# Attention scores of a head pair in two pieces instead of three, inside a fused attention and MLP kernel

## The chip, the cores and the metric

The kernel runs on one core of one Trainium2 chip. The metric is the device time of one execution in microseconds (us). The kernel before was timed three times: 943.04, 944.19 and 946.74 us, median 944.19 us.

## What is computed

The reference is causal attention with a window of 128 and a linear (ALiBi) bias, followed by an MLP with GELU:

```python
# q, k, v: 8 batches, 8 heads, 576 positions, 64 wide;  x: 4608 x 512
scores = scale * np.matmul(q, k.transpose(0, 1, 3, 2))
rel = pos[:, None] - pos[None, :]
bias = slopes[:, None, None] * (-np.abs(rel).astype(np.float32))[None, :, :]
mask = (rel >= 0) & (rel < window)
scores = np.where(mask, scores + bias[None], -1000000000.0)
scores = scores - np.max(scores, axis=-1, keepdims=True)
attn = np.exp(scores)
attn = attn / (np.sum(attn, axis=-1, keepdims=True) + 1e-09)
x = np.matmul(attn, v)          # reshaped to tokens x 512
h = x @ w_in                    # 512 x 2048
out = gelu(h) @ w_out           # 2048 x 512
```

## The kernel before

**Tiles.** The 4608 tokens are nine MLP tiles of 512. Every product is done in fp16 as a high and a low part, three matmuls for one. Tile `t` of the MLP is 32 steps: in steps 0 to 15 `mlp_in` forms one h of 128 features (12 matmuls of 512 columns, L600), the Activation engine (ACT) takes its GELU (L623), GpSimd (POOL) writes the high part (L625) and VectorE (DVE) the low part (`low_part`, L149); in steps 16 to 31 `mlp_out` forms a quarter of an output block `o` (again 12 matmuls, L661). The h and o tiles rotate through four PSUM buffers with the tag "mm". TensorE (PE) is kept on these products, and the attention of the next batch, `b = t + 1`, is threaded between the steps.

**Attention units.** A batch has four units, one for each pair of heads (0 to 3). A unit's scores need nine blocks of 64 rows per half, kept as nine groups in five PSUM banks (`BANKS`): (0, 1), (2, 3), (4,), (5, 6), (7, 8). A bank is called by its first group. Banks 0, 2 and 4 are the EVEN groups (five of them), banks 5 and 7 the ODD ones (four). A bank with two groups takes 12 matmuls of 64 x 64 by 192 columns, bank 4 takes 6 (L415). Each matmul uses one quadrant of the array: the head chooses the rows, the half the columns; bank 4 holds a group of both heads, one per half.

**What follows a score bank.** `scores` evicts each bank to SBUF on DVE, scaled and with the bias (L437), and POOL masks its head with a memset (L442). `softmax` does the EVEN groups, then the ODD ones: the row maximum on DVE (`nmax`, L507), one exponential per group on ACT (L510, given a priority by `EXP_AHEAD`; it needs another activation table than GELU, so a table load stands before and after each run of them), then on DVE the sum made ready (`z`, L513) and its reciprocal (L514), the high part of each group on POOL (`e_main`, L519), its low part on DVE (L149), and a transposing DMA to `et`. `weigh` multiplies `et` with v on PE (L559) into two PSUM tiles `av` (one for each MLP tile that the batch overlaps), and each is read by ACT (high part of x, L572) and by DVE (low part of x, L149).

**PSUM.** Score banks and `av` tiles rotate through four buffers with the tag "att", in the order in which they are allocated: a tile takes the buffer of the tile allocated four before it, and its first matmul waits until that one has been read for the last time.

**Order.** Units 0 to 3 of a batch begin their scores at the steps `SCORES_AT = (2, 11, 16, 21)`, and `weigh` follows at `WEIGH_AT = (12, 20, 25, 30)`. The scores are issued in three pieces (`PIECES`): banks 0 and 2 at step s, bank 4 at s + 1, banks 5 and 7 at s + 2, and then the softmax. In unit 0 of batches 3 to 6, step 6 issues `stat_v` for the next batch (L217, one long DVE reduction over v) and the scale computations after it (L119 to L144, DVE). The code gives the program order only. The framework's scheduler then orders the queue of each engine by its own model of time, so a change on PE also moves DVE, ACT, POOL and the DMA queue. Names such as `sc5_3_4` read: scores of batch 5, unit 3, bank 4; `av5_1_5` is the `av` of batch 5, unit 1, for MLP tile 5; `g32_2_6` is the GELU of tile 2, h 6.

Of the kernel before, what the change touches and what calls it, by code (L numbers as in the profile page):

```python
# [51 lines left out]
BANKS = ((0, 1), (2, 3), (4,), (5, 6), (7, 8))  # L52
IDLE = {0: 6, 5: 4}
PIECES = (slice(0, 2), slice(2, 3), slice(3, 5))


@with_exitstack
def attention_gelu_mlp(
# [15 lines left out]
    def small(shape, name, bufs, tag=None, dt=F32):  # L74
        return pool.tile(shape, dt, tag=tag or name, name=name, bufs=bufs)
# [231 lines left out]
    def load_v(b):  # L307
        v32 = pool.tile([P, NPAIR, NKB, P], F32, tag="v32", name=f"v32_{b}", bufs=1)
        for hp in range(NPAIR):
            nc.sync.dma_start(v32[:, hp], vp[b, hp].rearrange("(n p) d -> p n d", p=P))  # L310
        v32s[b] = v32
# [21 lines left out]
    def split_v(b):  # L333
        v32 = v32s.pop(b).rearrange("p h n d -> p (h n d)")
        hi = vbuf[:, 0].rearrange("p h n d -> p (h n d)")
        lo = vbuf[:, 1].rearrange("p h n d -> p (h n d)")
        nc.scalar.activation(hi, v32, AF.Copy, scale=scv[b])  # L337
        low_part(lo, v32, scv[b], hi)
# [44 lines left out]
    def bias_of(hp, head):  # L383
        return bias_p[:, hp : hp + 1, :] if head is None else bias_h[:, 2 * hp + head : 2 * hp + head + 1, :]

    def scores(st, banks):

        b, hp, u = st.b, st.hp, st.u
        if not hasattr(st, "s"):
            st.ps = {}  # L390
            st.s = pool.tile([P, NG, W], F32, tag="s", name=f"s{u}", bufs=2)
        s = st.s
        exact = b < EXACT
        terms = (None,) if exact else ((0, 0), (1, 0), (0, 1))

        def operands(term, r, j):
            q, k = slice(hp * S + j * QB, hp * S + (j + 1) * QB), slice(hp * S + PAD + (j - 2) * QB, hp * S + PAD + (j + 1) * QB)
            if exact:
                return qbuf32[r, q], kbuf32[r, k]
            return qbuf[r, term[0], q], kbuf[r, term[1], k]  # L400

        ps = st.ps
        for bank in banks:
            tag = "mm" if b == 0 and bank[0] in FIRST_MM else "att"
            ps[bank] = psum.tile([P, 2, 256], F32, tag=tag, name=f"sc{u}_{bank[0]}", bufs=4)
        for n in range(len(banks[0])):
            for i, term in enumerate(terms):
                for half in range(2):
                    for bank in banks:
                        head, j = GROUPS[bank[n]]  # L410
                        h = half if head is None else head
                        jj = j if head is None else j + 2 * half
                        r, o = slice(h * D, h * D + D), slice(half * D, half * D + D)
                        a, m = operands(term, r, jj)
                        nc.tensor.matmul(  # L415
                            ps[bank][o, n, 0:W], a, m, start=(i == 0), stop=(i == len(terms) - 1 and b > 0),
                            skip_group_check=True,
                        )
            if b == 0:
                for bank in banks:  # L420
                    adds = [(slice(0, W), ident, bias_of(hp, GROUPS[bank[n]][0])[:, 0])]
                    gap = (2 - GROUPS[bank[n]][1]) * QB
                    if gap > 0:

                        adds.append((slice(0, gap), upper, never[:, 0:gap]))
                    for i, (c, a, m) in enumerate(adds):
                        nc.tensor.matmul(
                            ps[bank][:, n, c], a, m, start=False, stop=(i == len(adds) - 1), skip_group_check=True
                        )
        if b == 0:  # L430
            return
        cs = csq[b]
        for bank in banks:
            head, k = GROUPS[bank[0]][0], len(bank)
            j = GROUPS[bank[0]][1]
            bias = bias_of(hp, head)
            nc.vector.scalar_tensor_tensor(  # L437
                out=s[:, bank[0] : bank[0] + k, :], in0=ps[bank][:, 0:k, 0:W], scalar=cs,
                in1=bias.broadcast_to([P, k, W]) if k > 1 else bias, op0=ALU.mult, op1=ALU.add,
            )  # L440
            if j < 2:
                nc.gpsimd.memset(s[0:D, bank[0], 0 : (2 - j) * QB], NEG)  # L442
# [136 lines left out]
    def tile_scales(t, ns):  # L579


        k = len(ns)
        r = slice(ns[0], ns[-1] + 1)
        gs = small([P, k], f"gs{t}_{ns[0]}", 4 if t == 0 else 2, tag=f"gs{k}")
        nc.vector.tensor_scalar(gs, pww[:, r], pwx[t], 2.0 ** -(24 if t >= FAST else 25), op0=ALU.mult, op1=ALU.mult)
        sg = small([P, k], f"sg{t}_{ns[0]}", 4 if t == 0 else 2, tag=f"sg{k}")
        nc.vector.tensor_scalar(sg, sww[:, r], sx[t], 2.0 ** -(22 if t >= FAST else 21), op0=ALU.mult, op1=ALU.mult)
        for n in ns:
            gsc[t, n], gsg[t, n] = gs[:, n - ns[0] : n - ns[0] + 1], sg[:, n - ns[0] : n - ns[0] + 1]
# [50 lines left out]
    def out_scale(t):  # L640
        so[t] = small([P, 1], f"so{t}", 2, tag="so")
        nc.vector.tensor_scalar(so[t], pwm, pwx[t], 2.0 ** -(14 if t >= FAST else 16), op0=ALU.mult, op1=ALU.mult)
# [101 lines left out]
    def sums_in_place():  # L744

        for d in range(NWP // 2):
            nc.sync.dma_start(wi[2 * d + 1][:, :, 0 : NCC : 2], stored[T1, d])
        for n in (T2, T3, T4):
            stream(n, 0)
# [216 lines left out]
    def unit(b, hp):  # L966
        if (b, hp) not in units:
            units[b, hp] = Unit(b, hp)
        return units[b, hp]

    def all_scores(st):
        for piece in PIECES:
            scores(st, BANKS[piece])
# [71 lines left out]
    scores_at, weigh_at, split_at = {1: 2, 4: 3}, {5: 0, 8: 1, 11: 2, 15: 3}, {1: 2, 3: 4, 5: 6}  # L1045
# [22 lines left out]
    for t in range(1, NTILE):  # L1068
        b = t + 1
        scores_at, weigh_at = (SCORES_AT, WEIGH_AT) if t > 1 else ((8, 14, 18, 22), (17, 22, 26, 30))  # L1070
        at = {s + i: (hp, i) for hp, s in enumerate(scores_at) for i in range(3)}
        tile_scales(t, range(NWP))
        out_scale(t)
        if t == FAST:
            seven_all(t)
            break
        for step in range(2 * NFC):
            if step < NFC:
                mlp_in(t, step)
            else:  # L1080
                tb, q = divmod(step - NFC, 4)
                for fc in range(4 * q, 4 * q + 4):
                    mlp_out(t, tb, fc)
            if t + 1 == FAST:
                if step in PARTS_AT:
                    parts.pop(0)()
                if step == NFC:
                    sums_in_place()
                if step in SUMS_AT:
                    sums_of_x(FAST, SUMS_AT.index(step))  # L1090
            if b >= B:
                continue
            if step in at:
                hp, i = at[step]
                scores(unit(b, hp), BANKS[PIECES[i]])
                if i == 2:
                    softmax(unit(b, hp))
            if step == 1:
                split_v(b)
                if b + 1 < B:  # L1100
                    load_v(b + 1)
                    load_qk(b + 1)
            if step == 6:
                if b + 1 < B:
                    stat_v(b + 1)
                else:

                    pwx[B] = pwv[B - 1]
                    sx[B] = small([P, 1], f"sx{B}", 3, tag="sx")
                    inverse(sx[B], pwx[B], 12)  # L1110
                    cx_last = small([P, 1], "cxl", 1)
                    nc.vector.tensor_scalar(cx_last, pwv[B - 1], sx[B], 2.0 ** -27, op0=ALU.mult, op1=ALU.mult)
            if step in weigh_at:
                weigh(unit(b, weigh_at.index(step)))
            if step == SCORES_AT[-1] + 3 and b + 1 < B:
                split_qk(b + 1)
        if t + 2 == FAST:
            room_for_sums()
            for n in range(4):

                parts.pop(0)(gate=unit(b, NPAIR - 1).z[:, NG - 1 : NG] if n < 2 else None)
# [36 lines left out]
```

## Time and profile before

| | before |
|---|---|
| median of three runs | 944.19 us |
| profiled execution | 947.36 us, its span 945.3 us |
| mean granted TensorE clock | 0.984 |
| PE busy | 909.2 us, 96% of the span |
| DVE busy | 720.3 us, 76% |
| ACT busy | 546.5 us, 58% |
| POOL busy | 194.2 us, 21% |
| score matmuls L415 | 1656, 74.3 us of PE's busy time |

All times below are microseconds from the span's start, as the profiled execution has them. A row of the timeline gives start, duration, engine, line, operation, what it writes and reads, shapes, the count of equal neighbours put into one row, and in square brackets the engine's idle time before it with what ended it. A row of windows gives, for a stretch of time, its length, the busy time of each engine, the clock that TensorE was granted, and the share and rate of the DMA engines. The profile drops the buffer numbers, so `s<-sc` is any eviction of a score bank.

### The profile page before, as it was taken

The numbers are of one execution on the slowest core, as the hardware profiler recorded it, in microseconds if no ns is written. First come the engines' busy times: TensorE is split into PE (matmuls) and PEld (weight loads), VectorE is DVE, ScalarE is ACT, GpSimd is POOL, SyncE is SP. The second block draws the span as 40 slices with busy tenths as digits, with TensorE's granted clock in tenths as the row PEclk, the third lists the DMA queues.
The fourth block names the chain that finished last, engine by engine and source line by source line (L and its number), as shares of the span: only waits on it lengthen the run. The fifth ranks groups of instructions, "written<-read, shape, count | busy, mean of one in ns | idle before, by whom it ended". The sixth has DMA issues, their size and how long they took to land.

```text
span 945.3 us, 18563 instructions
## 1 busy us (share of the span) xinstructions
PE 909.2 (96%) x7356; PEld 475.2 (50%) x7356; DVE 720.3 (76%) x1445; ACT 546.5 (58%) x1146; POOL 194.2 (21%) x412
## 2 busy tenths in 40 slices
PE   6969999789999899999999999999999999999998
PEld 3544444444454345444454445444544444445887
DVE  6798989779876877678767877787656799991771
ACT  5977967776673565356435643564465526731760
POOL 1010000013101443135313531163125420000000
PEclk9889999999999999999999999999999999999999
DMA  9518532972446124614562346225302554300201
GB/s 317 212 45 259 209 105 67 203 191 61 90 126 165 36 57 83 187 43 79 96 162 68 62 101 174 69 51 99 86 13 51 91 116 146 90 34 23 79 24 45
DMA packets 185527, 99.63 MB, mean 105 GB/s; under 512 B 133344, under 2 KB 165216, under 8 KB 185312
## 3 DMA queue, kind: packets, MB, share of 16 engines
q1 hardware_dynamic: 185440, 98.45, 41.3%
q8 instruction: 57, 0.93, 0.4%
q14 instruction: 30, 0.25, 0.1%
HBM read 50.72 MB, written 13.63 MB: 68 GB/s over the span
## 4 chain that ended last, share of the span: by engine, by line
PE 68%; DVE 7%; ACT 5%; DMA 4%; issue 2%; SPq 1%; DVEq 0%; ACTq 0%
PE o L661 31%; PE h L600 22%; PE av L559 4%; PE sc L415 4%; DMA v<-vp 2%; PE u L789 2%; PE u_out L901 2%; PE v L789 2%; DMA et<-e_main 1%; ACT s L510 1%; DVE stv L217 1%; DVE vbuf L149 1%; DVE nmax L507 1%; ACT L623 1%; ACT vbuf L337 1%
## 5 line engine op out<-in xcount | busy, mean ns | idle before, releaser
L600 PE MATMUL h<-x,wi 128*128 128x512 f16 x1536 | 344.7, 382 | 6.5 <-ACT g L623 3.0
L661 PE MATMUL o<-wo,g 128*128 128x512 f16 x1080 | 244.7, 379 | 1.1 <-DVE wo L149 1.1
L600 PEld LDWEIGHTS <-wi 128*128 128x128 f16 x1536 | 148.2, 98 | 188.0 <-issue 14.2
L661 PEld LDWEIGHTS <-g 128*128 128x128 f16 x1440 | 136.0, 98 | 164.6 <-issue 3.0
L510 ACT ACTIVATE s<-s,nmax 128x192 f32<-128x192 f32 x252 | 111.2, 443 | 103.1 <-DVE nmax L507 99.5
L623 ACT ACTIVATE g<-h,gs 128x512 f32<-128x512 f32 x112 | 74.8, 685 | 81.0 <-PE h L600 57.4
L149 DVE SCALAR_TENSOR_TENSOR g<-g,sg,g 128x512 f16<-128x512 f32 (+1 forms) x128 | 101.9, 811 | 22.6 <-POOL g L625 19.4
L625 POOL TENSOR_SCALAR g<-g,sg 128x512 f16<-128x512 f32 x96 | 78.5, 823 | 193.4 <-ACT g L623 189.6
L149 DVE SCALAR_TENSOR_TENSOR e_main<-s,z,e_main 128x192 f16<-128x192 f32 x252 | 107.4, 469 | 14.1 <-POOL e_main L519 9.6
L519 POOL TENSOR_SCALAR e_main<-s,z 128x192 f16<-128x192 f32 x180 | 87.6, 506 | 85.4 <-ACT s L510 29.0
L415 PE MATMUL sc<-kbuf,qbuf 64*64 64x192 f16 (+1 forms) x1656 | 74.3, 261 | 9.8 <-DMA kbuf<-kp 4.5
L661 PE MATMUL o<-wo_first,g 128*128 128x512 f16 x360 | 83.2, 380 | 0.3 <-DMA wo_first<-wo 0.3
L437 DVE SCALAR_TENSOR_TENSOR s<-sc,cs,bias_h 128x384 f32<-128x384 f32 x112 | 63.7, 607 | 12.8 <-PE sc L415 12.6
L507 DVE TENSOR_REDUCE nmax<-s 128x5 f32<-128x960 f32 (+1 forms) x56 | 58.5, 1044 | 2.2 <-POOL s L442 0.2
L442 POOL MEMSET s<- 64x128 f32 (+1 forms) x112 | 19.2, 172 | 186.4 <-DVE s L437 185.7
L572 ACT ACTIVATE x<-av,cx 128x448 f16<-128x448 f32 (+6 forms) x52 | 23.6, 474 | 58.4 <-PE av L559 58.2
L415 PEld LDWEIGHTS <-qbuf 64*64 64x64 f16 x1512 | 35.9, 106 | 38.2 <-issue 35.5
L559 PE MATMUL av<-et,vbuf 128*64 128x128 f16 (+1 forms) x1680 | 45.2, 213 | 4.2 <-DMA et<-e_main 4.2
L559 PEld LDWEIGHTS <-vbuf 128*64 128x64 f16 x1680 | 42.1, 113 | 14.3 <-issue 9.0
L510 ACT ACTIVATION_READ_ACCUMULATOR s<-s,nmax 128x1 f32 x252 | 47.2, 187 | 0.0
L510 ACT ACT_TABLE_LOAD x29 | 37.2, 1283 | 7.8 <-DVE square L120 7.3
L623 ACT ACT_TABLE_LOAD x29 | 37.2, 1283 | 6.4 <-issue 2.9
(224 smaller groups left out, 1029.0 us busy)
## 6 DMA issues: line engine op xcount, KB each, us to landing
v<-vp SPq DMA_DIRECT2D x32, 320.0 KB, 5.1
out<-ob SPq DMA_DIRECT2D x35, 256.0 KB, 2.2
raw<-w_in SPq DMA_DIRECT2D x8, 1024.0 KB, 14.0
raw<-w_out SPq DMA_DIRECT2D x8, 1024.0 KB, 5.7
q<-qp SPq DMA_DIRECT2D x7, 1152.0 KB, 6.1
k<-kp SPq DMA_DIRECT2D x7, 1152.0 KB, 6.6
stored<-ts SPq DMA_DIRECT2D x32, 128.0 KB, 2.2
room<-stored SPq DMA_DIRECT2D x12, 256.0 KB, 2.7
```

The lines of the kernel that those rows point to most:

```text
L149: nc.vector.scalar_tensor_tensor(out=dst, in0=src, scalar=scale, in1=high, op0=ALU.mult, op1=ALU.subtract)
L415: nc.tensor.matmul(ps[bank][o, n, 0:W], a, m, start=(i == 0), stop=(i == len(terms) - 1 and b > 0), skip_group_check=True,)
L437: nc.vector.scalar_tensor_tensor(out=s[:, bank[0] : bank[0] + k, :], in0=ps[bank][:, 0:k, 0:W], scalar=cs, in1=bias.broadcast_to([P, k, W] ...
L507: nc.vector.tensor_reduce(out=nmax[:, r], in_=s[:, r], axis=AX.X, op=ALU.max, negate=True)
L510: nc.scalar.activation(s[:, i, :], s[:, i, :], AF.Exp, bias=nmax[:, i : i + 1], accum_out=z[:, i : i + 1])
L519: nc.gpsimd.tensor_scalar(e[:, i, 0, c], s[:, i], z[:, i : i + 1], 1.0, op0=ALU.mult, op1=ALU.mult)
L559: nc.tensor.matmul(av[r, (j - blocks[0]) * QB : (j - blocks[0] + len(js)) * QB], v32s[b][:, hp, kb, r] if b < EXACT else vbuf[:, vi, hp, k ...
L600: nc.tensor.matmul(ph, wi[n][:, a, cc, k * P : (k + 1) * P], x[:, cc, b, :], start=(i == 0), stop=(i == 3 * NCC - 1),)
L623: nc.scalar.activation(g32, ph, AF.Gelu, scale=gsc[t, n])
L625: nc.gpsimd.tensor_scalar(g[:, r, 0], g32, gsg[t, n], 1.0, op0=ALU.mult, op1=ALU.mult)
L661: nc.tensor.matmul(o, both[:, a, c], wo[n][:, b, k, :], start=(fc == first and i == 0), stop=(fc == last and i == 2),)
L789: nc.tensor.matmul(ps[:, k * HT : (k + 1) * HT], w(a, i)[:, k * P : (k + 1) * P], m(b, i),  start=first and n == 0, stop=True, skip_group_ ...
```

## The change

From batch 3 on (five of the eight batches, 20 units) a unit's scores are issued in two pieces: banks 0, 2 and 4 at step s, banks 5 and 7 at step s + 2. Bank 4 thus comes one step earlier. Within the first piece the loop over group, term and half visits the three banks in turn, and skips bank 4 for the second group, which it doesn't have. Batches 1 and 2 keep three pieces. The number and kind of instructions is the same; lines of the changed kernel are one to four higher.

```diff
 PIECES = (slice(0, 2), slice(2, 3), slice(3, 5))
+PARTS = (slice(0, 3), slice(3, 5))
...
                     for bank in banks:
+                        if n == len(bank):
+                            continue
                         head, j = GROUPS[bank[n]]
...
-        at = {s + i: (hp, i) for hp, s in enumerate(scores_at) for i in range(3)}
+        parts_of = PARTS if b >= 3 else PIECES
+        at = {s + i * (4 - len(parts_of)): (hp, i) for hp, s in enumerate(scores_at) for i in range(len(parts_of))}
...
                 hp, i = at[step]
-                scores(unit(b, hp), BANKS[PIECES[i]])
-                if i == 2:
+                scores(unit(b, hp), BANKS[parts_of[i]])
+                if i + 1 == len(parts_of):
                     softmax(unit(b, hp))
```

The scheduler's queues change with it. The first place is DVE in unit 0 of batch 3, before: `stat_v` of batch 4 (`stv4`) stands ahead of bank 4 and of the EVEN maximum.

```order
412 L437 SCALAR_TENSOR_TENSOR s3_0_3438<-sc3_0_0_3439,cs3_3152,bias_h_63 128x384
413 L437 SCALAR_TENSOR_TENSOR s3_0_3438<-sc3_0_2_3440,cs3_3152,bias_h_63 128x384
414 L149 SCALAR_TENSOR_TENSOR g2_0_3388<-g32_2_2_3434,sg2_0_3371,g2_0_3388 128x512
415 L217 TENSOR_REDUCE stv4_3614<-v32_4_3412 128x1
416 L437 SCALAR_TENSOR_TENSOR s3_0_3438<-sc3_0_4_3486,cs3_3152,bias_p_64 128x192
417 L149 SCALAR_TENSOR_TENSOR g2_0_3388<-g32_2_3_3482,sg2_0_3371,g2_0_3388 128x512
418 L119 COPY quarters_3616<-stv4_3614 32x1 x4
419 L507 TENSOR_REDUCE nmax3_0_3542<-s3_0_3438 128x5
```

The same engine and place in the changed kernel:

```order
411 L440 SCALAR_TENSOR_TENSOR s3_0_3438<-sc3_0_4_3441,cs3_3152,bias_p_64 128x192
412 L150 SCALAR_TENSOR_TENSOR g2_0_3388<-g32_2_1_3406,sg2_0_3371,g2_0_3388 128x512
413 L440 SCALAR_TENSOR_TENSOR s3_0_3438<-sc3_0_0_3439,cs3_3152,bias_h_63 128x384
414 L440 SCALAR_TENSOR_TENSOR s3_0_3438<-sc3_0_2_3440,cs3_3152,bias_h_63 128x384
415 L150 SCALAR_TENSOR_TENSOR g2_0_3388<-g32_2_2_3434,sg2_0_3371,g2_0_3388 128x512
416 L510 TENSOR_REDUCE nmax3_0_3542<-s3_0_3438 128x5
417 L218 TENSOR_REDUCE stv4_3614<-v32_4_3412 128x1
418 L150 SCALAR_TENSOR_TENSOR g2_0_3388<-g32_2_3_3490,sg2_0_3371,g2_0_3388 128x512
```

Bank 4 is evicted first, and the EVEN maximum (128x5) has moved ahead of `stv4`.

The second place is DVE in unit 2 of batch 5, behind its EVEN maximum and up to the first `x` of `weigh(1)`. `e_main` is the low part of a group, `ob4_0` an eviction of an output block, `x5 <- av5_1_5` the last reader of that `av` tile. Before, the ODD banks were evicted just ahead of these rows:

```order
734 L513 TENSOR_SCALAR z5_2_6602<-z5_2_6602 128x5
735 L514 RECIPROCAL z5_2_6602<-z5_2_6602 128x5
736 L507 TENSOR_REDUCE nmax5_2_6601<-s5_2_6508 128x4
737 L149 SCALAR_TENSOR_TENSOR e_main_85<-s5_2_6508,z5_2_6602,e_main_85 128x192 x2
738 L671 TENSOR_SCALAR ob4_0_6651<-o4_0_6495,so4_5887 128x512
739 L149 SCALAR_TENSOR_TENSOR e_main_85<-s5_2_6508,z5_2_6602,e_main_85 128x192 x3
740 L513 TENSOR_SCALAR z5_2_6602<-z5_2_6602 128x4
741 L514 RECIPROCAL z5_2_6602<-z5_2_6602 128x4
742 L149 SCALAR_TENSOR_TENSOR e_main_85<-s5_2_6508,z5_2_6602,e_main_85 128x192 x2
743 L149 SCALAR_TENSOR_TENSOR x5_5128<-av5_1_5_6667,cx5_5_4925,x5_5128 128x192
```

In the changed kernel:

```order
729 L516 TENSOR_SCALAR z5_2_6602<-z5_2_6602 128x5
730 L517 RECIPROCAL z5_2_6602<-z5_2_6602 128x5
731 L150 SCALAR_TENSOR_TENSOR e_main_85<-s5_2_6508,z5_2_6602,e_main_85 128x192 x2
732 L440 SCALAR_TENSOR_TENSOR s5_2_6508<-sc5_2_5_6571,cs5_5666,bias_h_63 128x384
733 L440 SCALAR_TENSOR_TENSOR s5_2_6508<-sc5_2_7_6572,cs5_5666,bias_h_63 128x384
734 L150 SCALAR_TENSOR_TENSOR e_main_85<-s5_2_6508,z5_2_6602,e_main_85 128x192 x3
735 L510 TENSOR_REDUCE nmax5_2_6601<-s5_2_6508 128x4
736 L674 TENSOR_SCALAR ob4_0_6651<-o4_0_6495,so4_5887 128x512
737 L516 TENSOR_SCALAR z5_2_6602<-z5_2_6602 128x4
738 L517 RECIPROCAL z5_2_6602<-z5_2_6602 128x4
739 L150 SCALAR_TENSOR_TENSOR e_main_85<-s5_2_6508,z5_2_6602,e_main_85 128x192
740 L150 SCALAR_TENSOR_TENSOR x5_5128<-av5_1_5_6667,cx5_5_4925,x5_5128 128x192
```

The ODD banks and the ODD maximum (128x4) have moved from ahead of the EVEN low parts to between and behind them, and one ODD low part instead of two stands ahead of `x5`. In batch 3 two stand ahead of that `x`, in batch 4 one, in batches 6 and 7 none.

On PE the first piece of a unit goes to the banks 0, 2, 4, 0, 2, 4 and so on for 18 matmuls, then to 0, 2 for 12 more; before, bank 4 had its six behind the 12 matmuls of the next step. (In unit 3 of batches 3 and 4 alone the scheduler holds bank 4 back within the piece, behind eight and five matmuls of the others.) In both kernels the "att" tiles ahead of `sc5_3_4` are, in this order, `sc5_2_5`, `sc5_2_7`, `av5_1_5`, `av5_1_6`, `sc5_3_0`, `sc5_3_2`, so it takes the buffer of `av5_1_5`. The same holds in unit 3 of every batch: its bank 4 takes the buffer of the first `av` of `weigh(1)`, which step 20 has formed.

## Prediction

> **What bounds the kernel now.** I read the page first: busy time by engine, the chain that ended last, and the groups of the exponentials and of the score matmuls.
>
> ```profile
> PE 909.2 (96%) x7356; PEld 475.2 (50%) x7356; DVE 720.3 (76%) x1445; ACT 546.5 (58%) x1146; POOL 194.2 (21%) x412
> PE 68%; DVE 7%; ACT 5%; DMA 4%; issue 2%; SPq 1%; DVEq 0%; ACTq 0%
> L510 ACT ACTIVATE s<-s,nmax 128x192 f32<-128x192 f32 x252 | 111.2, 443 | 103.1 <-DVE nmax L507 99.5
> L415 PE MATMUL sc<-kbuf,qbuf 64*64 64x192 f16 (+1 forms) x1656 | 74.3, 261 | 9.8 <-DMA kbuf<-kp 4.5
> ```
>
> PE is busy for 96% of the span and carries 68% of the chain. So two things count: what leaves PE's queue, and what makes PE stand. The exponentials show the link behind it: of their 103.1 us of idle time ahead, 99.5 ended with a maximum from DVE. DVE's order decides when softmax runs, and that decides when buffers come free for PE.
>
> Next, PE's timeline in batch 5, from bank 4 of unit 2 to the first piece of unit 3 (some rows left out).
>
> ```profile
> 546.70 0.44 PE L415 MATMUL sc<-kbuf,qbuf 64*64 64x192 f16 x6
> 547.07 2.76 PE L661 MATMUL o<-wo,g 128*128 128x512 f16 x12
> 549.76 0.69 PE L415 MATMUL sc<-kbuf,qbuf 64*64 64x192 f16 x24
> 550.38 2.76 PE L661 MATMUL o<-wo,g 128*128 128x512 f16 x12
> 552.99 2.75 PE L661 MATMUL o<-wo_first,g 128*128 128x512 f16 x12
> ...
> 559.89 0.69 PE L415 MATMUL sc<-kbuf,qbuf 64*64 64x192 f16 x24
> ```
>
> PE goes from block to block without a hole, so a wait that the change puts at step 21 (559.89) adds to the time in full. The same rows price a piece: twelve output matmuls take 552.99 - 550.38 = 2.61; a piece of 24 takes 550.38 - 549.76 = 0.62 until the next block starts, one of 6 takes 547.07 - 546.70 = 0.37, and each visit is entered late by 549.76 - 547.07 - 2.61 = 0.08.
>
> **Part 1: one visit fewer, in 20 units.** Banks 0, 2 and 4 cost 0.70 + 0.45 in two visits; now it is one visit of 30 matmuls. The six cost at least their slope between the two sizes, 6 x (0.62 - 0.37)/18 = 0.08, and at most the 0.37 that they took alone. So a unit saves between 0.37 and 0.08, all units 7.4 to 1.6. A loss has no row that speaks for it. The order 0, 2, 4 lets one quadrant take two matmuls of each three, while before each took one in four, so I stay near the low end, 0.11 per unit: **-2.2 us**.
>
> A rule speaks against this part. The Trainium skill, "TensorE: Matmul & The Clock Gate", Part 3, says that a weight load overlaps matmuls in flight only if their row group differs; in each set of six the new order has two neighbours on the same rows. The trace disagrees: 24 pairs start within 0.62, so 0.026 apart, and a matmul lasts 0.26 (row of L415), so about ten are in flight, on both halves of the rows, whenever a load runs.
>
> **Part 2: the stall in batch 3.** Unit 0 of batch 3, first DVE, then ACT, then PE, and last the windows of the stall and of the slow stretch behind it (the 1.00 and the 0.51 are the granted clock).
>
> ```profile
> 307.65 2.82 DVE L217 TENSOR_REDUCE stv<-v 128x1 f32<-128x2560 f32 x1 [1.63 <-DMA v<-vp]
> 310.38 0.41 DVE L437 SCALAR_TENSOR_TENSOR s<-sc,cs,bias_p 128x192 f32<-128x192 f32 x1
> ...
> 312.00 1.16 DVE L507 TENSOR_REDUCE nmax<-s 128x5 f32<-128x960 f32 x1
> ```
>
> ```profile
> 323.32 1.84 ACT L623 ACTIVATE g<-h,gs 128x512 f32<-128x512 f32 x3
> ```
>
> ```profile
> 324.06 1.24 PE L600 MATMUL h<-x,wi 128*128 128x512 f16 x5 [2.43 <-ACT g L623]
> ```
>
> ```profile
> 321.25:324.06 2.81, 0.38 (x3) 0.10 (x1) 2.72 (x16) 2.78 (x7) 1.55 (x3) 1.00 0.00 0
> ...
> 325.35:328.80 3.45, 3.45 (x10) 1.25 (x9) 3.45 (x12) 0.69 (x1) 3.45 (x6) 0.51 0.82 152
> ```
>
> The reduction of `stat_v` holds DVE from 307.65 to 310.47. Bank 4 waits behind it, so the maximum ends at 313.16, the exponentials follow it, and the GELU that frees PSUM for PE comes at 323.32. PE stands for 2.43, then runs at half clock for 3.45, which loses 3.45 x 0.49 = 1.7: 4.1 in all. In the new order bank 4 and the EVEN maximum stand ahead of `stv4`. The maximum loses at least 2.82 + 0.41 of delay, and ACT moves with it by over 3 us, more than the 2.43 that PE waited. So the stall goes: **-4.1 us** (bounds -4.1 and 0). `stv4` and its scales now wait behind the maximum (1.16); they serve the next batch, and nobody waits for them so soon. If that cover were gone, it would cost those 1.16.
>
> **Part 3: a new wait at step 21.** Bank 4 of unit 3 takes the buffer of the first `av` of `weigh(1)`. Before, it was needed one step later, 2.61 + 0.70 = 3.3 after the piece began. Now the piece's third matmul needs it, and all of PE's queue stands behind. The rows of unit 2 in batch 5 on DVE, then ACT, say when the buffer is free.
>
> ```profile
> 550.36 1.15 DVE L507 TENSOR_REDUCE nmax<-s 128x5 f32<-128x960 f32 x1
> 551.43 1.13 DVE L437 SCALAR_TENSOR_TENSOR s<-sc,cs,bias_h 128x384 f32<-128x384 f32 x2
> ...
> 554.09 0.19 DVE L514 RECIPROCAL z<-z 128x5 f32<-128x5 f32 x1
> 554.20 0.91 DVE L507 TENSOR_REDUCE nmax<-s 128x4 f32<-128x768 f32 x1
> 555.02 0.94 DVE L149 SCALAR_TENSOR_TENSOR e_main<-s,z,e_main 128x192 f16<-128x192 f32 x2
> ...
> 556.55 1.06 DVE L149 SCALAR_TENSOR_TENSOR e_main<-s,z,e_main 128x192 f16<-128x192 f32 x3
> ...
> 559.52 0.41 DVE L149 SCALAR_TENSOR_TENSOR x<-av,cx,x 128x192 f16<-128x192 f32 x1
> ```
>
> ```profile
> 556.91 0.98 ACT L572 ACTIVATE x<-av,cx 128x192 f16<-128x192 f32 x2
> ```
>
> Before, the last reader, `x` low, ended at 559.93, just as unit 3 began. I chain the new order from the EVEN maximum, whose place behind the GELUs of tile 4 doesn't move (end 551.51): reciprocal done 554.28, two low parts until 555.96, the ODD banks 1.13 (557.1), three low parts 1.06 (558.1, less overlaps of 0.1), the ODD maximum 0.91 (558.9). From maximum to reciprocal the EVEN groups took 554.28 - 551.51 = 2.77; four exponentials instead of five make 2.77 - 0.44 = 2.33 (561.25). The first low part starts 555.02 - 554.28 = 0.74 behind it, for POOL's high part (561.99), takes 0.47 (562.46), and `x` low 0.41 more: about 562.8, or 11.3 behind the EVEN maximum. PE would wait 562.8 - 559.89 = 2.9. With no ODD low part ahead (batches 6 and 7) it is 561.25 + 0.41 and the hand-over, 10.2 behind; with two (batch 3) 0.5 more, 11.8. ACT's read of the same `av` (556.91) is done early in either order.
>
> The same two rows in batches 3, 4, 6 and 7, each from a narrow window of the timeline: first the EVEN maximum of unit 2, then where unit 3 began.
>
> ```profile
> 354.22 1.15 DVE L507 TENSOR_REDUCE nmax<-s 128x5 f32<-128x960 f32 x1
> 452.77 1.16 DVE L507 TENSOR_REDUCE nmax<-s 128x5 f32<-128x960 f32 x1
> 647.89 1.15 DVE L507 TENSOR_REDUCE nmax<-s 128x5 f32<-128x960 f32 x1
> 743.59 1.15 DVE L507 TENSOR_REDUCE nmax<-s 128x5 f32<-128x960 f32 x1
> ```
>
> ```profile
> 363.92 0.28 PE L415 MATMUL sc<-kbuf,qbuf 64*64 64x192 f16 x4
> 462.22 0.28 PE L415 MATMUL sc<-kbuf,qbuf 64*64 64x192 f16 x4
> 657.35 0.28 PE L415 MATMUL sc<-kbuf,qbuf 64*64 64x192 f16 x4
> 754.21 0.28 PE L415 MATMUL sc<-kbuf,qbuf 64*64 64x192 f16 x4
> ```
>
> Batch 3: 355.37 + 11.8 - 363.92 = 3.2, of which I take 2.2, since its softmax chain starts earlier than before. Batch 4: 453.93 + 11.3 - 462.22 = 3.0. Batch 6: 649.04 + 10.2 - 657.35 = 1.9. Batch 7: 744.74 + 10.2 - 754.21 = 0.7. With the 2.9 of batch 5: **+10.7 us** (bounds 0, if the low parts run as early as before, and 14).
>
> **Part 4: half clock behind the waits.** A stand of 2.43 was followed by 1.7 us of loss. Those of batches 4 and 5 are longer, so I count one slow stretch each: **+3.4 us** (bounds 0 and 6.8, four stretches). The Trainium skill, the same page, Part 1, says that the clock falls after at least one idle window of about 3.4 us; by that none of these waits would cost a stretch, and the sum would be the second rival's. The row of 2.43 speaks against the rule.
>
> The other moved rows (unit 0's and unit 1's evictions, GELUs and exponentials changing places) exchange small waits that I take as nothing in sum, with 2 us to either side.
>
> **Sum.** -2.2 - 4.1 + 10.7 + 3.4 = +7.8, so the profiled 947.36 would become 955.2. The median of the runs is 944.19; with the same difference it is **952.0**.
>
> **Rivals.**
> - *The waits don't come* (1 in 10): DVE reaches `x` low before step 21, as it nearly did before (559.93 against 559.89), because the ODD maximum isn't the last link. Then only parts 1 and 2 are left: -6.3, 937.9. It decides if `x` low ends within 8.4 us of the EVEN maximum. The order, with the maximum behind five low parts, speaks against it.
> - *Waits without slow stretches* (1 in 4): +4.4, 948.6. The waits may be shared out over two clock windows; the skill's rule would give this too. It is within what counts as no change.
> - *More of it* (1 in 10): the stall in batch 3 stays, since its GELUs now meet the exponentials elsewhere, or four stretches are slow: +12, 956.
> - *Weight loads don't overlap on the same rows* (1 in 50): 6 neighbours a unit at the load's share, 475.2/7356 = 0.065 each, in 20 units: 7.8 on top, 959.8. The rows above speak against it.
>
> **The numbers.** My forecast (waits and two slow stretches) has about 0.53. A measurement of this kernel tells about 0.5% (4.7 us) from no change. Slower by more: the forecast nearly whole, the third and fourth rival, and a part of the second: 0.64. Within 0.5%: most of the second, and the forecast's low end: 0.26. Faster: 0.10. The range leaves out the first rival and reaches down to waits of half the size with the stall gone (-6.3 + 5.4 = -0.9, 943), and up to four stretches with the stall still there (+15, 959).
>
> **What would show it.** Right: in the trace after, the EVEN maximum of unit 0 in batch 3 ends ahead of the 2.8 us reduction and PE's gap at 321 is gone; PE stands ahead of the third score matmul of unit 3 in batches 3 to 6, released by DVE's `x`, for 2 to 3 us, with a granted clock of 0.5 behind some of them; a first piece takes about 0.97 instead of 0.62 + 0.37 and the second entry. Wrong: unit 3's pieces start and finish without a hole, or the longest gaps stand elsewhere, at GELU's or unit 0's banks.

## The result, and the profile after

The changed kernel took 956.57 us in the median of four runs (954.77 to 957.22), the kernel before 944.95 (943.04 to 946.74): a ratio of 1.0123, with a 95% interval of 1.0102 to 1.0144. The change cost 11.6 us.

The profiled executions differ by less, 956.25 against 947.36. That of before lies 2.4 above its median, and it lost that time ahead of the change: compared matmul by matmul, the first h of tile 2, which both kernels reach by the same code, came 3.8 us earlier in the changed kernel's trace. From there to the end the changed kernel lost 12.9.

The page of the changed kernel, in the lines that answer to those of before:

```profile
PE 906.0 (95%) x7356; PEld 476.0 (50%) x7356; DVE 724.7 (76%) x1445; ACT 544.0 (57%) x1146; POOL 191.4 (20%) x412
L513 ACT ACTIVATE s<-s,nmax 128x192 f32<-128x192 f32 x252 | 111.1, 442 | 125.6 <-DVE nmax L510 121.5
L418 PE MATMUL sc<-kbuf,qbuf 64*64 64x192 f16 (+1 forms) x1656 | 70.0, 259 | 21.8 <-DVE x L150 12.3
```

PE is busy for 3.2 us less and yet the kernel is longer. The exponentials wait 121.5 us for a maximum, 22 more than before. The score matmuls have a new releaser, `x` on DVE, with 12.3 us of PE's idle time. PE's timeline through units 2 and 3 of batch 5 shows where:

```profile
543.59 0.94 PE L418 MATMUL sc<-kbuf,qbuf 64*64 64x192 f16 x30
544.46 5.35 PE L664 MATMUL o<-wo,g 128*128 128x512 f16 x24
549.75 0.69 PE L418 MATMUL sc<-kbuf,qbuf 64*64 64x192 f16 x24
...
557.18 2.76 PE L664 MATMUL o<-wo,g 128*128 128x512 f16 x12
559.87 0.27 PE L418 MATMUL sc<-kbuf,qbuf 64*64 64x192 f16 x2
563.19 0.93 PE L418 MATMUL sc<-kbuf,qbuf 64*64 64x192 f16 x28 [3.05 <-DVE x L150]
```

In unit 2 the piece of 30 runs through in 544.46 - 543.59 = 0.87. In unit 3 PE issues two of the 30, to banks 0 and 2, and stands for 3.05 at the third. DVE's rows of the same time, from unit 2's EVEN maximum on, say what it stands for:

```profile
550.81 1.15 DVE L510 TENSOR_REDUCE nmax<-s 128x5 f32<-128x960 f32 x1 [0.29 <-POOL s L445]
...
555.35 1.07 DVE L150 SCALAR_TENSOR_TENSOR e_main<-s,z,e_main 128x192 f16<-128x192 f32 x2 [0.62 <-POOL e_main L522]
556.33 1.13 DVE L440 SCALAR_TENSOR_TENSOR s<-sc,cs,bias_h 128x384 f32<-128x384 f32 x2
557.39 1.06 DVE L150 SCALAR_TENSOR_TENSOR e_main<-s,z,e_main 128x192 f16<-128x192 f32 x3
558.37 0.94 DVE L510 TENSOR_REDUCE nmax<-s 128x4 f32<-128x768 f32 x1
...
562.24 0.57 DVE L150 SCALAR_TENSOR_TENSOR e_main<-s,z,e_main 128x192 f16<-128x192 f32 x1 [0.62 <-POOL e_main L522]
562.73 0.41 DVE L150 SCALAR_TENSOR_TENSOR x<-av,cx,x 128x192 f16<-128x192 f32 x1
```

`x` low ends at 563.14, 11.2 behind the end of the EVEN maximum (551.96), and PE goes on at 563.19. Behind such waits comes a slow stretch in batches 3 and 4, but not in 5. Two windows of batch 3 (the wait, then the slow stretch):

```profile
355.60:359.25 3.65, 0.05 (x4) 0.00 (x0) 1.93 (x6) 1.81 (x8) 1.81 (x4) 1.00 1.02 226
...
360.20:363.60 3.40, 3.40 (x10) 1.21 (x9) 2.58 (x5) 0.44 (x2) 0.40 (x2) 0.51 0.81 154
```

Unit 0 of batch 3 on DVE shows the other half of the forecast. The EVEN maximum ends at 303.28, and `stat_v`'s reduction comes after it:

```profile
299.33 0.41 DVE L440 SCALAR_TENSOR_TENSOR s<-sc,cs,bias_p 128x192 f32<-128x192 f32 x1
...
302.14 1.14 DVE L510 TENSOR_REDUCE nmax<-s 128x5 f32<-128x960 f32 x1
304.10 2.82 DVE L218 TENSOR_REDUCE stv<-v 128x1 f32<-128x2560 f32 x1 [0.81 <-DMA v<-vp]
```

PE's gap at h 10 of that tile is gone. Other gaps have come: at the last weigh of a batch (here in batch 5), at h 9 of tile 5, and within the first h of tile 7:

```profile
591.68 1.60 PE L562 MATMUL av<-et,vbuf 128*64 128x128 f16 x66 [1.14 <-DMA et<-e_main]
...
622.22 2.10 PE L603 MATMUL h<-x,wi 128*128 128x512 f16 x9 [1.77 <-ACT g L626]
...
796.66 1.67 PE L603 MATMUL h<-x,wi 128*128 128x512 f16 x7 [1.87 <-DVE x L150]
```

Comparing the start of the first matmul of each h and o block in the two traces splits the 12.9 us:

| where | changed minus before, us |
|---|---|
| the stall of batch 3 | -4.4 |
| unit 0 of batch 4 (smaller gaps) | -1.4 |
| step 21 in batches 3 to 7, with the slow stretches, and less the visits saved in unit 3 | 5.25 + 5.03 + 3.09 + 1.34 + 1.10 = 15.8 |
| the last weigh | 2.2 |
| h 9 of tile 5 | 1.8 |
| first h of tile 7 | 2.0 |
| the rest: visits saved in units 0 to 2 | -3.1 |

### The profile page after: what moved, and what is told of

The parts are those of the page before. It is cut to its first block, busy times and chain, and to the rows that moved or that the text cites. A ratio compares the mean times of both kernels' runs of the same rounds, so it can differ in the third digit from the quotient of the medians.

```text
span 954.4 us, 18541 instructions
## 1 busy us (share of the span) xinstructions
PE 906.0 (95%) x7356; PEld 476.0 (50%) x7356; DVE 724.7 (76%) x1445; ACT 544.0 (57%) x1146; POOL 191.4 (20%) x412
## 5 line engine op out<-in xcount | busy, mean ns | idle before, releaser
L664 PE MATMUL o<-wo,g 128*128 128x512 f16 x1080 | 247.9, 385 | 0.5 <-DVE wo L150 0.5
L603 PEld LDWEIGHTS <-wi 128*128 128x128 f16 x1536 | 148.2, 98 | 189.2 <-issue 13.9
L664 PEld LDWEIGHTS <-g 128*128 128x128 f16 x1440 | 138.3, 99 | 168.8 <-issue 9.3
L513 ACT ACTIVATE s<-s,nmax 128x192 f32<-128x192 f32 x252 | 111.1, 442 | 125.6 <-DVE nmax L510 121.5
L150 DVE SCALAR_TENSOR_TENSOR e_main<-s,z,e_main 128x192 f16<-128x192 f32 x252 | 112.9, 494 | 18.3 <-POOL e_main L522 13.7
L150 DVE SCALAR_TENSOR_TENSOR g<-g,sg,g 128x512 f16<-128x512 f32 (+1 forms) x128 | 99.3, 790 | 19.1 <-POOL g L628 16.7
L418 PE MATMUL sc<-kbuf,qbuf 64*64 64x192 f16 (+1 forms) x1656 | 70.0, 259 | 21.8 <-DVE x L150 12.3
L516 DVE TENSOR_SCALAR z<-z 128x5 f32<-128x5 f32 (+1 forms) x56 | 9.3, 166 | 56.4 <-ACT s L513 56.2
```

What stands on the lines that cost most here:

```text
L150: nc.vector.scalar_tensor_tensor(out=dst, in0=src, scalar=scale, in1=high, op0=ALU.mult, op1=ALU.subtract)
L418: nc.tensor.matmul(ps[bank][o, n, 0:W], a, m, start=(i == 0), stop=(i == len(terms) - 1 and b > 0), skip_group_check=True,)
L513: nc.scalar.activation(s[:, i, :], s[:, i, :], AF.Exp, bias=nmax[:, i : i + 1], accum_out=z[:, i : i + 1])
L603: nc.tensor.matmul(ph, wi[n][:, a, cc, k * P : (k + 1) * P], x[:, cc, b, :], start=(i == 0), stop=(i == 3 * NCC - 1),)
L664: nc.tensor.matmul(o, both[:, a, c], wo[n][:, b, k, :], start=(fc == first and i == 0), stop=(fc == last and i == 2),)
```

## The experiments

The first theory was the prediction's: bank 4 of unit 3 needs, one step earlier, a buffer that DVE reads late. Both are needed, the early bank and the late reader. Rival A blames the later ODD softmax wherever the next reader stands, rival B the rotation of buffers alone, and rival C doubts that unit 0's order made the stall of batch 3. The edits are against the changed kernel where not said otherwise. "Gaps" are sums over the five batches, worked out as the time from one matmul's start to the next one's, less the usual 0.216.

### Two pieces in some units only

`parts_of` is chosen per unit, with the condition `hp < 3`, `hp == 3`, `hp < 2` or `hp == 0` in place of all units; for the last run `b == 3 and hp == 0` (the lines that use `parts_of` are left out here):

```diff
-        parts_of = PARTS if b >= 3 else PIECES
+        parts_of = [PARTS if b >= 3 and hp < 3 else PIECES for hp in range(NPAIR)]
...
```

> Units 0 to 2 of batches 3 to 7 in two pieces, unit 3 in three as before. My theory (bank 4 of unit 3, a step earlier, needs a buffer that DVE reads late): bank 4 is needed 3.3 us later again, so the five waits at step 21 (12.5 us in the trace of the changed kernel) and the two slow stretches (3.4) go, and the waits for et of unit 3 in batches 3 and 5 (2.1) and for x ahead of the last tile (2.0) go with unit 3's old order; the stall of batch 3 stays away: 956.6 - 15.8 - 4.1 + 0.8 for five visits = about 937.5, range 936 to 941. Rival A (the later ODD softmax of units 0 to 2 is what costs, wherever the next reader stands): the waits reappear at step 22 or at weigh, 947 or more.

Measured: 938.94 us (before, on the same chip, 943.57; ratio 0.9948, interval 0.9925 to 0.9971). Unit 2's order is that of the changed kernel, its ODD maximum late; but bank 4 is needed at step 22 again, and only 0.9 us of gaps are left there. The gaps at the last weigh did not go: 0.7, 0.9 and 1.4 in batches 3 to 5. That part of the expectation failed, and there rival A has a point.

> Only unit 3 of batches 3 to 7 in two pieces. The buffer that bank 4 takes is the same as in the changed kernel, but unit 2's DVE order is that of before, where the last reader of that buffer ended within 0.1 us of step 21. My theory (both are needed: early bank and late reader): waits at step 21 of at most 0.5 each, the stall of batch 3 (4.1) stays, and unit 3's own later ODD softmax keeps its 4.1 at weigh and at the last tile: 945.0 + 4.1 - 0.8 = about 948, range 945 to 951. Rival B (the rotation of buffers alone makes the wait): 15.8 more than before, about 960.

Measured: 945.05 (ratio 1.0013, 0.9997 to 1.0028). Bank 4 is early and takes the same buffer, the reader is early too, and the piece of unit 3 in batch 5 has no hole:

```profile
554.36 0.94 PE L418 MATMUL sc<-kbuf,qbuf 64*64 64x192 f16 x30
555.23 1.04 PE L664 MATMUL o<-wo,g 128*128 128x512 f16 x4
```

Only batch 3 waited at step 21, for 0.85. Rival B is out. The gaps at the last weigh are here as well (0.85, 1.1 and 0.95), and come with unit 3's two pieces, the only thing that is new. Part of them is PE's own queue: here, as in the changed kernel, nine, eight and nine output matmuls stand between the last weigh of batches 3 to 5 and the next tile's first h, where before there were four, three and four. The weigh comes five of them (5 x 0.216 = 1.1 us) earlier. The gap at h 9 of tile 5 comes with unit 3 as well (1.3); the one at tile 7, which the expectation had here too, does not.

> Units 0 and 1 of batches 3 to 7 in two pieces, units 2 and 3 in three. My theory: no wait at step 21, unit 2's order as before; what stays of the change is the stall of batch 3 gone (-4.4), the smaller stall of batch 4 (-1.4), a new one at h 9 of tile 5 (+1.8) and ten visits (-1.5): 945.0 - 5.5 = about 939.5, range 937 to 942. Rival C (the stall of batch 3 came from something other than unit 0's order, and moves elsewhere): 944 to 946.

Measured: 937.43 (ratio 0.9921, 0.9903 to 0.9939). No gap at step 21 or at the last weigh.

> Only unit 0 of batches 3 to 7 in two pieces. My theory: as units 0 and 1 together (937.4), but without unit 1's five visits of 0.1 to 0.2: 938 to 939; all of the gain beyond visits is in unit 0. Rival: the gain needs unit 1 too (its banks free earlier): 941 or more.

Measured: 937.07 against 943.41 (ratio 0.9932, 0.991 to 0.9954). Unit 1 adds nothing that the runs can tell.

> Only unit 0 of batch 3 in two pieces: the EVEN maximum then stands ahead of the long reduction on DVE, and one visit is saved. My theory (that reduction ahead of bank 4 made the stall of batch 3): the gap of 2.4 us at h 10 of tile 2 goes, and the slow stretch where there was one: 943.6 - 0.2 - 2.4 to 4.1 = 939 to 941. Rival C (the stall moves on to a later h or comes from elsewhere): no change, 943 to 945.

Measured: 938.68 (ratio 0.9952, 0.9935 to 0.9968). In this trace PE runs through the place of the stall:

```profile
310.76 11.60 PE L603 MATMUL h<-x,wi 128*128 128x512 f16 x53
```

One unit of twenty brings 4.7 of the 6.3 us that unit 0 of all five batches brings. Rival C is out.

### The reader earlier, by an earlier weigh

```diff
-    SCORES_AT, WEIGH_AT = (2, 11, 16, 21), (12, 20, 25, 30)
+    SCORES_AT, WEIGH_AT = (2, 11, 16, 21), (12, 19, 25, 30)
```

> The changed kernel with the second weigh one step earlier (19 instead of 20). In the queue that this gives, the last reader of its first av on DVE stands right behind the ODD maximum and the output eviction, ahead of the second reciprocal and low parts, 2.8 us earlier; bank 4 and its buffer are as in the changed kernel. My theory: the waits at step 21 fall from 12.5 to under 2.5 and the slow stretches go, the other new waits (5.9) stay: 956.6 - 13.5 = about 943, range 941 to 946. Rival B (the rotation alone, or PE's own order in the piece): 955 to 957 as the changed kernel. Rival A: 950 or more.

Measured: 952.3 (ratio 1.0084, 1.0067 to 1.0101), 9 us above the expectation, and in the range of rival A. The waits at step 21 did fall, to 1.9 and 2.3 in batches 3 and 4 and none in the others, 4.2 for 12.5. But the gaps at the last weigh grew from 2.3 to 6.7, as here in batch 5, and three slow stretches came where none was expected:

```profile
585.80 2.45 PE L562 MATMUL av<-et,vbuf 128*64 128x128 f16 x58 [3.28 <-DMA et<-e_main]
```

So the wait had been found in the right place, but mending it there brought less than expected, since part of it came back later.

### The buffer free earlier, by a copy

The first `av` of the second weigh goes to SBUF, and `x` is formed from there:

```diff
-            nc.scalar.activation(x[:, 0], av[:, :n], AF.Copy, scale=c)
-            low_part(x[:, 1], av[:, :n], c, x[:, 0])
+            src = av[:, :n]
+            if b >= 3 and hp == 1 and t == b:
+                src = pool.tile([P, TT], F32, tag="ob", name=f"avc{st.u}", bufs=3)[:, :n]
+                nc.scalar.copy(src, av[:, :n])
+            nc.scalar.activation(x[:, 0], src, AF.Copy, scale=c)
+            low_part(x[:, 1], src, c, x[:, 0])
```

> The changed kernel, but the first av of the second weigh is copied to SBUF by ACT (behind the ODD exponentials, some 0.4 us), and ACT and DVE form x from the copy; the copy takes a place in the rotation of the output tiles. The buffer that bank 4 takes is then free 1.5 us earlier, no longer by DVE. My theory: the waits at step 21 are released by ACT's copy and fall from 12.5 to about 5.5, the slow stretches mostly go: 956.6 - 7 - 1.7 to 3.4 = 945 to 949. Rival B (DVE's read isn't the release that counts): 955 to 958.

Measured: 956.28 against 943.41 (ratio 1.0142, 1.0117 to 1.0167): no gain. That is the time which rival B foretold, but not its mechanism: at step 21 everything came as expected, with ACT's copy as the releaser and 5.3 us of gaps for 12.5. The groups of PE's score and weigh matmuls in this trace, and in the changed kernel's below it:

```profile
L418 PE MATMUL sc<-kbuf,qbuf 64*64 64x192 f16 x1512 | 50.7, 247 | 7.7 <-ACT avc L578 5.0 <-DVE s L440 1.4 <-ACT kbuf L373 0.6
L562 PE MATMUL av<-et,vbuf 128*64 128x128 f16 x1008 | 43.1, 229 | 12.9 <-DMA et<-e_main 12.8
```

```profile
L418 PE MATMUL sc<-kbuf,qbuf 64*64 64x192 f16 x1512 | 50.6, 247 | 14.1 <-DVE x L150 12.3 <-DVE s L440 1.2 <-DVE kbuf L150 0.5
L562 PE MATMUL av<-et,vbuf 128*64 128x128 f16 x1008 | 40.2, 221 | 6.1 <-DMA et<-e_main 6.0
```

12.3 + 6.0 became 5.0 + 12.8. What PE no longer waited for at step 21 it waited for at the last weigh. (This trace also has three slow stretches, two behind that weigh and one at tile 7, where the changed kernel's has two.) Batch 4's DVE in the run with the copy shows what stands ahead of that weigh:

```profile
469.99 0.94 DVE L510 TENSOR_REDUCE nmax<-s 128x4 f32<-128x768 f32 x1
470.86 2.60 DVE L150 SCALAR_TENSOR_TENSOR kbuf<-k,scq,kbuf 128x2304 f16<-128x2304 f32 x1
473.38 2.60 DVE L150 SCALAR_TENSOR_TENSOR qbuf<-q,scq,qbuf 128x2304 f16<-128x2304 f32 x1
...
479.92 2.55 DVE L218 TENSOR_REDUCE stq<-q 128x1 f32<-128x2304 f32 x1 [1.73 <-DMA q<-qp]
482.39 1.07 DVE L150 SCALAR_TENSOR_TENSOR e_main<-s,z,e_main 128x192 f16<-128x192 f32 x3
```

Unit 3's ODD maximum, too, stands behind all its EVEN low parts, and behind it stand the low parts of the next batch's k and q. The load of the q after that waits for their buffers, its statistic (2.55) for the load, and the last ODD low parts, which the weigh needs, for the statistic. The statistic stood ahead of those low parts in the kernel before, too; what differs is the time that is left until PE comes. PE's and DVE's rows of batch 4 before:

```profile
483.76 7.29 PE L661 MATMUL o<-wo,g 128*128 128x512 f16 x33
490.98 1.20 PE L559 MATMUL av<-et,vbuf 128*64 128x128 f16 x38
```

```profile
484.29 1.40 DVE L149 SCALAR_TENSOR_TENSOR e_main<-s,z,e_main 128x192 f16<-128x192 f32 x4
```

and PE's in the run with the copy:

```profile
478.59 6.21 PE L668 MATMUL o<-wo,g 128*128 128x512 f16 x28
487.91 2.35 PE L562 MATMUL av<-et,vbuf 128*64 128x128 f16 x44 [3.12 <-DMA et<-e_main]
```

Before, the low parts ended at 485.69, 5.3 ahead of the weigh, and nothing waited. With the copy they end at 483.46, and PE, which has five output matmuls fewer ahead of the weigh, is there at 487.91 - 3.12 = 484.79, only 1.3 later. So the first theory had the place of the wait and half of its cause. The second theory is rival A with a cause: unit 2's and unit 3's softmax chains on DVE end late, and PE meets them at the first thing that depends on them, the buffer at step 21 or `et` at the last weigh.

### Bank 4 behind the others in the same step

```diff
-                scores(unit(b, hp), BANKS[parts_of[i]])
+                for piece in (PIECES[0:2] if parts_of is PARTS and i == 0 else (parts_of[i],)):
+                    scores(unit(b, hp), BANKS[piece])
```

> The changed kernel, but with bank 4's six matmuls behind the 24 of banks 0 and 2 in the same step, and its eviction last; unit 2's DVE order behind its EVEN maximum is that of the changed kernel. My theory: the waits at step 21 stay, shorter only by the 0.5 us of the matmuls that now run ahead of them (12.5 to about 10), the first piece costs 0.62 + 0.2 to 0.37 instead of 0.87: 953 to 957. Rival D (evicting bank 4 first is what turned DVE's order and made the waits): the waits go, 940 to 945.

Measured: 957.32 (ratio 1.0155, 1.0124 to 1.0186), 0.3 above the expected range. 9.2 us of gaps at step 21, 4.2 at the last weigh. DVE evicts bank 4 last here and the waits stay, so rival D is out; and what the waits at step 21 lost (3.3) was again paid in part at the last weigh (1.9).

### The second piece one step after the first

In all units:

```diff
-        at = {s + i * (4 - len(parts_of)): (hp, i) for hp, s in enumerate(scores_at) for i in range(len(parts_of))}
+        at = {s + i: (hp, i) for hp, s in enumerate(scores_at) for i in range(len(parts_of))}
```

> The changed kernel with banks 5 and 7 at step s + 1 instead of s + 2, in all four units. In the queue that this gives, the ODD banks and the ODD maximum stand ahead of the EVEN low parts again; bank 4 and its buffer are as in the changed kernel. My second theory (after the copy of av, which moved the waits from step 21 to the last weigh): units 2 and 3 end their softmax some 3 us late because the ODD maximum stands behind the EVEN low parts, and PE meets that at step 21 or, if it is let past, at the weigh of unit 3 and at the next tile. Then the waits go in all three places: x low about 9.1 us behind the EVEN maximum instead of 11.2, so at most 0.8 per batch at step 21 (3 in all instead of 12.5), nothing at weigh and at the last tile, no slow stretch: 956.6 - 12 to 18 = 938 to 944. Rival E (the early bank 4 of the two-piece form holds the buffers too long, whatever DVE's order): 950 or more.

Measured: 940.39 against 942.55 (ratio 0.9973, 0.996 to 0.9985). Bank 4 is where the changed kernel has it, on the same buffer, and no batch waits at step 21. Unit 3 of batch 5:

```profile
553.55 0.94 PE L418 MATMUL sc<-kbuf,qbuf 64*64 64x192 f16 x30
554.43 2.76 PE L664 MATMUL o<-wo,g 128*128 128x512 f16 x12
```

At the last weigh 1.6, 2.1 and 0.7 are left in batches 3 to 5, where the expectation had none, and unit 0's bank 7 now waits 0.5 to 0.9 in batches 4 to 6. Rival E, that an early bank 4 costs by itself, is out.

The same, with both pieces one step later:

> Two pieces, but at s + 1 and s + 2: bank 4 at the step that it had before, banks 0 and 2 a step later. DVE's order in unit 2 is that of before (the ODD maximum ahead of the EVEN low parts); in unit 0 of batch 3 the long reduction stands ahead of the EVEN maximum as before. My second theory: nothing waits at step 22 or at weigh by over 1, the visits save 20 x 0.17 to 0.2 = 3.5, and the stall of batch 3 stays: 939 to 943. Rival E (two pieces cost by themselves): 945 or more.

Here the steps are s + 1 and s + 2 (`s + i + 3 - len(parts_of)`). Measured: 945.34 (ratio 1.0023, 1.0005 to 1.0041), over the expectation, and the time that rival E had foretold; by this run alone rival E would stand, and it is the run before, at 940.39, that rules it out. Nothing waits at step 22 or at the last weigh, as expected, and the stall of batch 3 didn't come, which I had not expected; but the gain is eaten, for the most part by gaps in units 0 and 1: up to 1.4 at unit 0's bank 7 and at h 10 of tiles 3 and 4, and 1.2 at the first weigh of batch 3.

The second piece a step after the first in units 2 and 3 alone (`s + i * (4 - len(parts_of) if hp < 2 else 1)`):

> Units 0 and 1 as in the changed kernel (second piece at s + 2, which gave 937.4), units 2 and 3 with the second piece at s + 1. My second theory: the gain of units 0 and 1 stays (about 6), units 2 and 3 add their ten visits (1.7 to 2) and lose at most 3 at step 21: 936 to 940. Rival E: 948 or more.

Measured: 949.52 (ratio 1.0064, 1.0045 to 1.0082), a miss by 10, and again a time that rival E had foretold. The wait moved to another place, unit 2's bank 7 at step 17, 1.2 to 1.9 in each batch (7.7 in all, with slow stretches in batches 3 and 4), and at the last weigh 1.6, 1.7 and 0.6 stand in batches 3 to 5:

```profile
L418 PE MATMUL sc<-kbuf,qbuf 64*64 64x192 f16 x1512 | 52.0, 247 | 9.2 <-DVE s L440 8.4 <-DVE kbuf L150 0.5 <-ACT kbuf L373 0.2
```

Its releaser is an eviction. In the built program bank 7 of unit 2 has the PSUM bank of bank 4 of the same unit: buffers go on in the order in which the scheduler sees them come free, not strictly to the fourth tile after, as I said ahead of the prediction (for unit 3's bank 4 both give the `av` tile). DVE evicts bank 4 only when unit 1's softmax has run, which ends late since unit 1 kept the second piece at s + 2. By these rows it is the second theory's mechanism one unit earlier, and I hadn't looked for it there; no run isolates it.

### The order of DVE alone

One tiny operation makes unit 2's EVEN reciprocals depend on the ODD maximum, so that it can't stand behind the EVEN low parts:

```diff
-            nc.vector.tensor_reduce(out=nmax[:, r], in_=s[:, r], axis=AX.X, op=ALU.max, negate=True)
+            first = st.b >= 3 and st.hp == 2
+            if not (first and r is ODD):
+                nc.vector.tensor_reduce(out=nmax[:, r], in_=s[:, r], axis=AX.X, op=ALU.max, negate=True)
...
             nc.vector.reciprocal(z[:, r], z[:, r])
+            if first and r is EVEN:
+                nc.vector.tensor_reduce(out=nmax[:, ODD], in_=s[:, ODD], axis=AX.X, op=ALU.max, negate=True)
+                nc.vector.scalar_tensor_tensor(
+                    out=z[:, EVEN], in0=nmax[:, NG - 1 : NG].broadcast_to([P, NEVEN]), scalar=0.0, in1=z[:, EVEN],
+                    op0=ALU.mult, op1=ALU.add,
+                )
```

> The changed kernel with one more tiny DVE operation in unit 2 of batches 3 to 7, which makes the EVEN reciprocals depend on the ODD maximum (it adds zero times that maximum), so that the ODD maximum has to stand ahead of the EVEN low parts. Pieces, steps, banks and buffers are those of the changed kernel, unit 3's order too. Second theory (the softmax chain of unit 2, through DVE's order, is what PE waits for, at step 21 or later): x low comes about 9.5 us behind the EVEN maximum instead of 11.2, unit 3's softmax starts about 2 us earlier, the waits at step 21 fall from 12.5 to 4 to 5 and the time with them, since the last weigh doesn't wait longer: 956.6 - 8 - up to 3.4 for slow stretches = 945 to 949. That is the same relief at step 21 as by the copy of av (5.3), which gave no time back. Rival E (early bank 4, whatever DVE's order) or the first theory's buffer alone (relief at step 21 moves on to the weigh of unit 3 again): 955 to 957.

Measured: 949.2 against 942.98 (ratio 1.0057, 1.0034 to 1.0081), 0.2 above the expected range.

```profile
L418 PE MATMUL sc<-kbuf,qbuf 64*64 64x192 f16 x1512 | 50.7, 247 | 10.7 <-DVE x L150 8.3 <-DVE s L440 1.8 <-DVE kbuf L150 0.5
L570 PE MATMUL av<-et,vbuf 128*64 128x128 f16 x1008 | 40.7, 222 | 5.0 <-DMA et<-e_main 5.0
```

The relief at step 21 is smaller than by the copy (8.3 for 12.3, where I had expected 4 to 5; in batch 5 `x` low ends 10.0 behind the EVEN maximum, for 11.2), but nothing of it is given back at the last weigh (5.0 for 6.0), and the time fell by 7.4 (by 6.2, if each is set against its own runs of the kernel before). One slow stretch is left of two.

The chain itself can be measured, from the end of unit 2's EVEN maximum to the end of unit 3's last ODD low part, as the mean of batches 3 to 5:

| kernel | chain, us |
|---|---|
| before | 32.0 |
| unit 3 in two pieces | 32.4 |
| second piece a step after the first | 32.9 |
| units 0 to 2 in two pieces | 33.2 |
| ODD maximum first in unit 2 | 34.0 |
| second weigh at step 19 | 34.6 |
| `av` copied | 35.4 |
| changed | 35.6 |
| changed, bank 4 behind the others | 35.8 |

The longer chain is not made by PE's wait itself: its first half, up to unit 3's EVEN maximum, takes 13.9 before, 15.7 in the changed kernel, and 15.9 with the copy, where PE waited less than half as long at step 21.

The copy frees the buffer and leaves the chain nearly as it was, and no time comes back. Where the chain is shorter, time comes back: with the earlier weigh 4.3 (2.9, each against its own runs of before), with the ODD maximum first 7.4. That is the second theory against the first.

## Why the prediction was right

It forecast a loss of 7.8 us (952.0, range 943 to 959) and the loss was 11.6. Point by point:

- **Part 1, the visits.** 2.2 forecast. A piece of 30 costs 0.87 where two visits cost 0.62 + 0.37 and the second entry's 0.08: 0.20 saved per unit, 4.0 in 20 (in the table 3.1 of it is the last row, the rest stands in the row of step 21). The size was off; the truth lies in the middle of the bounds. The six extra matmuls cost 0.25, 0.042 each, which is above the 0.026 of a full piece and below what an exposed load (0.065) would make of them. So the rule of the fourth rival did not bind here.
- **Part 2, the stall.** 4.1 forecast, 4.4 measured in the two traces, for the reason given; unit 0 of batch 3 alone shows it.
- **Part 3, the wait at step 21.** 10.7 forecast, 12.5 measured. In batch 5 `x` low ended 11.2 behind the EVEN maximum, where 11.3 was worked out. By batches 3.6, 3.3, 3.1, 1.4 and 1.1 came, where 2.2, 3.0, 2.9, 1.9 and 0.7 were forecast; batch 3's discount for an earlier chain had no row behind it, and did not come. In batches 3 and 4 PE stood ahead of the ninth and the sixth matmul of the piece, not the third, as the scheduler had put bank 4 there.
- **Part 4, slow stretches.** Two forecast, two came (15.8 - 12.5 = 3.3). The number was right by luck: they came in batches 3 and 4, where 4 and 5 were forecast, and the wait of batch 5 fell on two clock windows, as the second rival had it (last section).
- **What failed:** "the other moved rows exchange small waits that I take as nothing in sum, with 2 us to either side". They made 2.2 + 1.8 + 2.0 - 1.4 = 4.6. The 2.2 at the last weigh and the 2.0 at tile 7 are ends of the same late softmax chain, which I followed only to its first reader; PE's own queue, with the last weigh five output matmuls earlier, adds to the 2.2. The 1.8 at h 9 of tile 5 comes with unit 3's two pieces. With the two ends counted as they measured, the sum would have been +12.
- **The size of the cause.** The prediction has the buffer as the thing waited for. The copy shows that it is only where PE first meets a late chain, 3.6 us longer than before (35.6 for 32.0). That half of the explanation was wrong, though it changed no number of the forecast.
- **The base.** The profiled execution of before lost 3.8 ahead of the first changed unit and was 2.4 above its median, so the difference of profiles (8.9) understates that of medians.

Left open: what makes the gaps at the last weigh in the run with the second piece a step after the first, where the last ODD low part ends 6 us or more ahead of the weigh (mostly 4.4 to 4.6 where the weigh waits with the second piece at s + 2). The trace puts them down to the transfer of `et`, and no run separates the transfers queued there.

The best versions are those with unit 0, or units 0 and 1, in two pieces: 937.07 and 937.43, 0.7 to 0.8% under the runs of the kernel before beside them.

## What to carry to other kernels

Merging two pieces of work on the busiest engine saves its entry cost, here 0.2 us a piece, but it also brings a buffer's next user forward and lets the scheduler reorder every engine behind it; the reordering was worth 4.4 us for the change in one place and 15.8 against it in another, where the visits saved 4.0. A wait for a buffer may show only where a late chain is met, as here, and not what makes it late: free the buffer and look whether the time falls, before believing in the buffer. And a change that is good in some units and bad in others is found by applying it to one unit at a time.

## What the runs showed of the hardware

A stand of PE of the same length brings a slow stretch in one execution and not in another. The stall of batch 3 was 2.43 us in the trace of before and was followed by 3.45 us at a granted clock of 0.51; in the run with two pieces in unit 3 only, PE stood 2.43 for the same GELU and went on at 1.00. The changed kernel's wait of 3.05 in batch 5 brought none:

```profile
319.13 3.18 PE L603 MATMUL h<-x,wi 128*128 128x512 f16 x14 [2.43 <-ACT g L626]
```

```profile
320.40:323.90 3.50, 3.50 (x18) 1.57 (x17) 3.50 (x12) 0.69 (x1) 3.50 (x6) 1.00 0.81 151
```

```profile
563.19:566.60 3.41, 3.41 (x40) 1.91 (x40) 3.12 (x8) 0.00 (x0) 0.88 (x3) 1.00 0.46 104
```

What divides the cases can be read from the traces afterwards. In each of them the slow stretches begin on one grid of 3.41 us (the two of the changed kernel, at 360.2 and 462.6, lie 30 such windows apart), and what counts is how long PE was idle within one window. The stall of before left 3.41 - 1.31 = 2.1 us of idle time in one window (the first row below); the equal stall in the run with unit 3 only was divided into 1.8 and 0.6 (the next two), and the wait of 3.05 in the changed kernel into 1.5 and 1.6 (the last two):

```profile
321.96:325.37 3.41, 1.31 (x7) 0.60 (x7) 2.62 (x14) 3.17 (x5) 2.11 (x5) 1.00 0.20 40
```

```profile
315.10:318.51 3.41, 1.61 (x8) 0.62 (x7) 3.27 (x16) 3.37 (x11) 2.77 (x4) 1.00 0.00 0
318.51:321.92 3.41, 2.79 (x13) 1.26 (x13) 2.66 (x12) 2.42 (x4) 2.74 (x5) 1.00 0.70 133
```

```profile
558.21:561.62 3.41, 1.93 (x11) 0.72 (x9) 2.10 (x5) 2.27 (x10) 0.00 (x0) 1.00 0.63 119
561.62:565.03 3.41, 1.84 (x33) 1.22 (x33) 2.79 (x9) 0.36 (x1) 1.89 (x4) 1.00 0.60 150
```

From 240 us on, leaving out the last 7 us, the 14 traces have nine windows at full clock with 2.1 us or more of idle PE, and half clock followed each of them; it followed five of ten between 1.66 and 1.97, and none below. A forecast doesn't know where the grid will lie, so a slow stretch behind a stand of 2 to 3.5 us is a matter of chance in it, worth 1.7 us each time that it comes.
